# Attention joined to a mixture of experts: another order of work where the last heads meet the first expert

## The chip, the cores and the metric

The kernel runs on one core of one Trainium2 chip. The metric is the device time of one execution in microseconds. The engines of the core are TensorE (PE, and PEld for its weight loads), VectorE (DVE), ScalarE (ACT), GpSimd (POOL) and SyncE (SP); each executes its own instructions in the order in which they were written.

## The reference

Causal attention with a forgetting bias comes first, and its output rows are the input of eight experts, of which each row takes one:

```python
scores = scale * np.matmul(q, k.transpose(0, 1, 3, 2))          # q, k, v: 8 x 8 x 576 x 64
cum = np.cumsum(np.maximum(s, 0.0), axis=-1)
bias = -(cum[:, :, :, None] - cum[:, :, None, :])
scores = np.where(causal, -1000000000.0, scores + np.minimum(bias, 0.0))
attn = np.exp(scores - np.max(scores, axis=-1, keepdims=True))
attn = attn / (np.sum(attn, axis=-1, keepdims=True) + 1e-09)
x = np.matmul(attn, v).transpose(0, 2, 1, 3).reshape(4608, 512)
...
logits = xn @ en.T / tau                                        # normed rows, 8 experts
expert_idx = np.argmax(logits, axis=1)
gate_w = probs[np.arange(N), expert_idx]                        # softmax of the logits
for e in range(8):
    h = np.maximum(x[mask] @ w1[e], 0.0)                        # 512 -> 1024
    out[mask] = gate_w[mask, None] * (h @ w2[e])                # 1024 -> 512
```

## The kernel before

Every operand of a matmul that needs more than 16 bits is kept as a high and a low part, and each product is three matmuls. So an exponential P has a remainder PL (the function `pl_`, line 235 on POOL and line 488 on DVE), v has vh (ACT, line 292) and vl (DVE, line 293), a weight has a converted half (`wcv`, ACT, line 804) and a remainder (`wlow`, DVE, line 812), a row of x has xH (ACT, line 741) and xL (DVE, line 743), and the hidden layer has a Relu (ACT, line 833) and its remainder (DVE, line 834; its tiles are called hv, hp and hq).

**Attention** is a software pipeline, `step(n)`, one step for each of the 64 heads (NH = 64) and a few steps around them. Step n computes the scores of head n on PE (tiles ta and tb), their exponentials on ACT (`expa`, line 478, and `expb1`, line 481), the conversion of v, and the product P times v of head n - 2 (`pv`, 15 triples of matmuls, 128 x 73 each, into the PSUM tile om, lines 506 to 508). The three DVE instructions `norm1` to `norm3` (lines 519, 523, 531) divide om by the row sums into xt. There is one tile om, so `pv` of a head waits until `norm3` of the head before it has read om; `norm1` of head n - 3 stands at the beginning of step n.

After the last head of a batch the **router** (`router`, lines 575 to 659) picks each row's expert in a queue of small DVE tasks (`sume`, `sel1` to `sel5`), PE ranks the rows (`rank0`), DVE computes their places (`rank1` to `rank3`, `rows`), and POOL scatters the rows to the DRAM table xs (`scat`, line 645, five for a batch). `slot()` takes one task from the queue, `scatter()` one scatter.

**Experts**: `xload` gathers 128 rows from xs (POOL, line 705), `xprep` transposes them on PE (line 736, four matmuls) and splits them into xH and xL; `l1(m, e, lo, hi)` computes one of eight slices of the hidden layer (line 824), `l2(e, t)` one tile of 128 rows of the output (line 848, 24 matmuls). `l1` has two PSUM buffers: slice m + 2 waits until DVE has taken the remainder of slice m out of PSUM. `wsq` sums squares of weights on ACT (line 776), `wnorm` (lines 787 to 794) makes a scale from the sums with one matmul and six small DVE instructions, and raw weights arrive by DMA in tiles that `wlow` gives free. The first three row tiles of expert 0 (SPL = 384 rows) are known early; its other two tiles, t = 3 and 4, need the scatters of the last two batches.

**The joint** is steps 62 to 66 and the code behind them. In step 63 (n = NH - 1) come the transposes of the three early row tiles; `tail(n)` puts `l1(0)`, `l1(1)`, `l1(2)` into steps 64 to 66, ahead of `pv` of heads 62 and 63; then follow `l1(3)` to `l1(7)`, three `l2`, and within them `third` and `fourth` (the row tiles 3 and 4), and then the rest of expert 0, in which a second `gate` (lines 77 to 104: norm, logits, exps, weight) is computed after the slices m = 1, 3, 5 and 7. All order is that of the written code.

Of the kernel before, what the change touches and what calls it, by code (L numbers as in the profile page):

```python
# [106 lines left out]
def main(ctx, tc, qkh, qkc, vtin, s_in, emb, tau, w1h, w2h, out, shared, nb):  # L107
# [402 lines left out]
    def norm1(n):  # L510
        if not 0 <= n < NH:
            return
        b, hh = n // H, n % H
        o = HD[n]["o"]
        if hh == 0:
            XT[b] = p2.tile([128, 5, XR], F32, name="xt", bufs=2)
        z = HD[n]["z"] = p2.tile([128, 5], F32, name="z")
        ov = HD[n]["ov"] = o[:, 0:365].rearrange("p (j c) -> p j c", c=73)
        nc.vector.tensor_scalar(z, ov[:, :, 72 * (hh % 2)], 1.0e-9 * 2.0 ** PSH, 2.0 ** XSH, op0=ALU.add, op1=ALU.mult)

    def norm2(n):
        if 0 <= n < NH:
            nc.vector.reciprocal(HD[n]["z"], HD[n]["z"])

    def norm3(n):
        if not 0 <= n < NH:
            return
        b, hh = n // H, n % H
        xt, z, ov = XT[b], HD[n]["z"], HD[n]["ov"]
        o = 72 * hh  # L530
        nc.vector.tensor_tensor(xt[:, :, o:o + 72], ov[:, :, 1 - hh % 2:73 - hh % 2], z.unsqueeze(2).to_broadcast([128, 5, 72]), op=ALU.mult)  # L531
        del HD[n]
        if hh == H - 1:
            nc.gpsimd.tensor_copy(xt[:, :, XW:XR].bitcast(I32), IX["recf"][:, b].unsqueeze(2).to_broadcast([128, 5, XR - XW]))
            nc.gpsimd.tensor_copy(xt[:, :, XW + 1:XW + 3], VB[b]["ws"].unsqueeze(1).to_broadcast([128, 5, 2]))
            router(b, xt)
# [38 lines left out]
    def router(b, xt):  # L575
# [17 lines left out]
        def sel4():  # L593
            R["w"] = om[:, 500:505]
            nc.vector.tensor_reduce(R["w"], R["T"], AX.X, ALU.max)
# [122 lines left out]
    def xprep(e, t, pt=None, info=True):  # L718
# [3 lines left out]
        if e + t // (SPL // 128) > 0 and not isinstance(X[("L", e)], tuple):  # L722
            X[("L", e)] = (X[("L", e)], p2.tile([128, 4, CAP], F16, tag="xt", name="xL", bufs=2))
        x = X[("r", e, t)][:, 0:XW]
# [10 lines left out]
        for c in range(4):  # L735
            nc.tensor.transpose(out=pt[:, 128 * c:128 * c + 128], in_=x[:, 144 * c + 8:144 * c + 136], identity=ident)
        if info:
            xstat(e, t)
        pv = pt.rearrange("p (c t) -> p c t", c=4)
        xH = X[("H", e)][:, :, 128 * t:128 * t + 128]  # L740
        nc.scalar.copy(xH, pv)
        xL = X[("L", e)] if e + t // (SPL // 128) == 0 else X[("L", e)][1]
        nc.vector.tensor_tensor(xL[:, :, 128 * t:128 * t + 128], pv, xH, op=ALU.subtract)  # L743
# [65 lines left out]
    def wlow():  # L809
        while lows:  # L810
# [90 lines left out]
    def step(n):  # L901
# [70 lines left out]
        wlow()  # L972
# [25 lines left out]
        tail(n)  # L998
# [7 lines left out]
        if n == NH - 1:  # L1006
            xprep(0, 2, pxs(), False)
        pv(n - 2, [3, 4])
        if live:
# [10 lines left out]
        if live:  # L1020
            prep(n, False)
            if n:
                vcp(n, True)
        if k > 0:
# [3 lines left out]
        slots(4)  # L1028
# [8 lines left out]
        for _ in range(SCN[c8] if n < NH - 22 else 1 + (c8 > 5) + 4 * (n > NH - 6)):  # L1037
            scatter()
# [9 lines left out]
    def PS(n):  # L1048
        return 1600 if n < NH - 6 else 1024

    def tail(n):
# [16 lines left out]
        if k == 7:  # L1068
            for t in range(2):
                xprep(0, t, pxs(), False)  # L1070
# [31 lines left out]
    for m in range(3, 8):  # L1102
        l1(m, 0, 0, SPL, partial(some, 12) if m == 5 else wnorm if m == 4 else None)
        if m == 3:
            wlow()
            some(12)
# [4 lines left out]
        if m > 5:  # L1111
            some(0)
# [4 lines left out]
    xinfo(0, SPL // 128, NTL)  # L1117
    for t in range(SPL // 128, NTL):
        xload(0, t)
# [19 lines left out]
    l2(0, 1)  # L1139
    wsq(24)  # L1140
    l2(0, 2, {4: third, 7: fourth})
    for e in range(NE):
        nx = e + 1 < NE
        w2, w1 = 16 * e + 8, 16 * e + 16
        for m in range(8):
# [26 lines left out]
            if e == 0 and m % 2:  # L1172
                X[("g", 0, SPL // 128)][m // 2]()
# [162 lines left out]
```

## Time and profile before

| | |
|---|---|
| median of 3 runs | 790.39 us (789.15 to 791.65) |
| the profiled execution | 791.17 us, of which the span from the first to the last instruction is 789.5 us |
| PE busy | 764.2 us, 97% of the span |
| DVE, ACT, POOL busy | 527.9, 566.5, 382.8 us |
| TensorE's granted clock, mean | 0.991 of full speed |

A row of a timeline has the start of an instruction in us from the start of the span, its length, engine, line, operation, output and inputs, shape and count, and in brackets the idle time of the engine ahead of it with what ended it. Attention ends and the experts begin between 343 and 420 us.

### The profile page before, as it was taken

To read this page: it belongs to the slowest core of one execution; us is meant where nothing else is said; L and a number is where in the kernel's file an instruction comes from. 1 tells how busy PE (TensorE), PEld (TensorE's weight loads), DVE (VectorE), ACT (ScalarE), POOL (GpSimd) and SP (SyncE) were. 2 spreads that over 40 slices of the span, in tenths; PEclk is the share of its full clock that TensorE was granted. 3 is DMA by queue.
4 is the path that set the end of the run, shared out by engine and by line. 5 is a ranking of instruction groups with operands and counts; after the bars stand their busy time and mean duration, and the time that the engine had idled before them with its cause. 6 is when DMAs were issued, how large, how long until landed. Compare 5 with 4: busy or idle time off the path is not lost. (4 is left out here: it accounts for less than half of the span.)

```text
span 789.5 us, 19448 instructions
## 1 busy us (share of the span) xinstructions
PE 764.2 (97%) x7290; PEld 570.3 (72%) x7290; DVE 527.9 (67%) x1784; ACT 566.5 (72%) x1010; POOL 382.8 (48%) x369
## 2 busy tenths in 40 slices
PE   8799999999999999987999999999999999999997
PEld 4699999999999999975476647556465574664753
DVE  7767888888888888877565756555664565556621
ACT  6699989898989898966556866837747567476410
POOL 8767798989898979771432121230221212302001
PEclk9899999999999999999999999999999999999999
DMA  8897879797979796770635665564754657635001
GB/s 160 195 210 134 180 172 212 169 212 172 212 170 217 176 196 177 180 256 28 207 88 162 163 202 158 143 183 122 185 181 113 177 154 147 194 106 131 24 15 54
DMA packets 76896, 125.03 MB, mean 158 GB/s; under 512 B 38960, under 2 KB 39364, under 8 KB 75934
## 3 DMA queue, kind: packets, MB, share of 16 engines
q0 software_dynamic: 20240, 70.92, 38.5%
q1 hardware_dynamic: 56560, 52.84, 24.6%
q8 instruction: 58, 0.95, 0.5%
q14 instruction: 38, 0.31, 0.1%
HBM read 95.23 MB, written 21.49 MB: 148 GB/s over the span
## 5 line engine op out<-in xcount | busy, mean ns | idle before, releaser
L235 POOL TENSOR_TENSOR PL<-P 128x576 f16<-128x576 f32 (+2 forms) x128 | 203.4, 1695 | 19.0 <-ACT P L478 10.6
L824 PEld LDWEIGHTS <-wt 128*128 128x128 f16 x1536 | 150.0, 98 | 63.2 <-issue 4.8
L824 PE MATMUL h<-xH,wt 128*128 128x320 f16 (+2 forms) x1024 | 187.8, 299 | 2.5 <-DVE hq L834 1.8
L854 POOL DMA_INDIRECT out<-Kx,xj x39 | 40.3, 1034 | 162.5 <-DVE Kx L853 112.4
L705 POOL DMA_INDIRECT Qx<-xs,idx x40 | 43.2, 1080 | 143.7 <-ACT hp L833 84.8
L506 PE MATMUL om<-vh,P 128*128 128x73 f16 x960 | 107.9, 199 | 3.4 <-DVE xt L531 3.0
L508 PE MATMUL om<-vh,PL 128*128 128x73 f16 x960 | 107.1, 198 | 0.9 <-POOL PL L235 0.9
L507 PE MATMUL om<-vl,P 128*128 128x72 f16 x960 | 107.3, 197 | 0.0
L824 PE MATMUL h<-xL,wt 128*128 128x320 f16 (+1 forms) x480 | 106.1, 297 | 0.5 <-DVE xL L743 0.5
L343 PE MATMUL s<-qkb 96*128 96x288 f32 (+4 forms) x270 | 96.8, 372 | 2.3 <-DVE M L351 1.1
L507 PEld LDWEIGHTS <-P 128*128 128x128 bf16 x960 | 95.2, 99 | 4.5 <-issue 4.1
L508 PEld LDWEIGHTS <-PL 128*128 128x128 f16 x960 | 94.3, 98 | 1.2 <-POOL PL L235 1.2
L848 PE MATMUL pxs<-wt,hp 128*128 128x512 f16 x351 | 94.9, 379 | 0.0
L506 PEld LDWEIGHTS <-P 128*128 128x128 bf16 x960 | 94.2, 99 | 0.2
L848 PE MATMUL pxs<-wt,hq 128*128 128x512 f16 x351 | 88.6, 379 | 0.0
L351 DVE CUSTOM_DVE_ANT_0 junk<-s,mS 128x320 bf16<-128x320 f32 (+3 forms) x142 | 73.3, 524 | 4.9 <-PE s L343 3.4
L853 DVE TENSOR_SCALAR Kx<-pxs,xj,idx 128x512 f32<-128x512 f32 x39 | 31.5, 808 | 55.7 <-PE pxs L848 39.9
L481 ACT ACTIVATE P<-tb 128x1024 f32<-128x1024 f32 x64 | 65.2, 1018 | 3.5 <-PE tb L448 2.5
L445 PE MATMUL tb<-QC,KC 128*128 128x448 f32 (+3 forms) x256 | 64.3, 309 | 0.0
L848 PEld LDWEIGHTS <-hp 128*128 128x128 f16 x351 | 34.3, 98 | 41.5
L848 PEld LDWEIGHTS <-hq 128*128 128x128 f16 x351 | 34.3, 98 | 41.3
L833 ACT ACTIVATE hv<-h 128x640 f16<-128x640 f32 (+2 forms) x18 | 11.6, 645 | 72.6 <-PE h L824 63.4
(239 smaller groups left out, 1845.0 us busy)
## 6 DMA issues: line engine op xcount, KB each, us to landing
qkb<-qkh POOLq DMA_DIRECT2D x15, 1216.0 KB, 9.2
ring<-w2h SPq DMA_DIRECT2D x44, 256.0 KB
ring<-w1h SPq DMA_DIRECT2D x36, 256.0 KB
vT<-vtin SPq DMA_DIRECT2D x28, 320.0 KB
KC<-qkh POOLq DMA_DIRECT2D x15, 576.0 KB, 9.1
QC<-qkh POOLq DMA_DIRECT2D x15, 576.0 KB, 8.2
rw<-w1h SPq DMA_DIRECT2D x15, 256.0 KB
rw<-w2h SPq DMA_DIRECT2D x12, 256.0 KB
```

What stands on the lines that cost most here:

```text
L235: nc.gpsimd.tensor_tensor(out, a, b_, op=ALU.subtract)
L343: nc.tensor.matmul(out, G[g]["QB"][0:96, h, 128 * i:128 * i + 128], G[g]["KB"][0:96, h, lo:hi], start=True, stop=True)
L351: nc.vector.tensor_tensor_reduce(out=jk, in0=src, in1=ms, scale=1.0, scalar=NEG, op0=ALU.add, op1=ALU.max, accum_out=MP[n // 2][:, n % 2, ...
L445: nc.tensor.matmul(out, HD[n]["KC"][:, ks:ks + 128], HD[n]["QC"][:, qlo:qhi], start=False, stop=stop)
L481: nc.scalar.activation(HD[n]["P32"][:, 576:1600], HD[n]["tb"], AF.Exp, scale=0.125)
L506: nc.tensor.matmul(out, lh, vh[:, kb], start=(kb == 0), stop=False)
L507: nc.tensor.matmul(out[:, u:u + 72], lh, vl[:, kb], start=False, stop=False)
L508: nc.tensor.matmul(out, ll, vh[:, kb], start=False, stop=(kb == j))
L705: ins = nc.gpsimd.indirect_dma_start(out=x.bitcast(I32), out_offset=None, in_=src, in_offset=bass.IndirectOffsetOnAxis(ap=X[("i", e, t)][1 ...
L824: nc.tensor.matmul(h[:, u, 0:b - a], w[:, 128 * c:128 * c + 128], x[:, c, lo + a:lo + b], start=(c == 0 and k == 0), stop=(c == 3 and k == 2))
L848: nc.tensor.matmul(y, h[:, 128 * t:128 * t + 128], w, start=(m == 0 and k == 0), stop=(m == 7 and k == 2))
L854: nc.gpsimd.indirect_dma_start(out=out, out_offset=bass.IndirectOffsetOnAxis(ap=xf[0].bitcast(U32), axis=0), in_=ys, in_offset=None, bound ...
```

## The change

It rewrites the joint. In step 63 the second exponential of head 63, the conversion of v and the matmuls of `pv(61)` stand ahead of the row conversions (`xprep` is cut into `xtr`, the transposes, and `xcv`, the conversions). The norms of heads 61, 62 and 63 follow their own `pv` at once instead of standing in the next step. The weight remainders of steps 63 and 64 are taken together, four of them, behind the norm of head 62; those of steps 64 and 65 stand behind `l1(3)`. `PS` now gives all of the remainder PL of heads 62 and 63 to POOL; before, 576 of its 1600 columns were DVE's. The five scatters of batch 6 move from the end of step 62 to the end of step 64. `l1(0)` to `l1(2)` stand behind the `pv` of their step. The router of the last batch takes its tasks in steps 65 and 66 and inside `l1(3)`, not inside and behind `l1(3)` to `l1(5)`. Its PSUM columns move (500:505 to 496:501), so that they no longer overlap those of `wnorm`. The gathers of row tiles 3 and 4 stand behind `l1(4)` and `l1(5)`, `third` in the second `l2` and `fourth` earlier in the third one. The second gate's parts come after slices 1, 4, 5 and 7.

```diff
@@ -508,7 +508,7 @@
     def norm1(n):
-        if not 0 <= n < NH:
+        if n not in HD:
             return
...
@@ -591,7 +591,7 @@
             nc.vector.tensor_tensor(R["T"], R["T"], wval, op=ALU.mult)
 
         def sel4():
-            R["w"] = om[:, 500:505]
+            R["w"] = om[:, 496:501]
             nc.vector.tensor_reduce(R["w"], R["T"], AX.X, ALU.max)
 
         def sel5():
@@ -715,12 +715,29 @@
         nc.scalar.activation(P32J[:, 0:DM].rearrange("p (q d) -> p q d", q=4), x.rearrange("p (q c) -> p q c", q=4)[:, :, 8:136], AF.Square, accum_out=ss)
         esum(nc, L, x.unsqueeze(1))
 
-    def xprep(e, t, pt=None, info=True):
+    def xset(e, t):
         if ("H", e) not in X:
             X[("H", e)] = const.tile([128, 4, CAP], F16, tag=f"vT{e % 2}", name="xH")
             X[("L", e)] = WT[1][:, 8192:8192 + 4 * SPL].rearrange("p (c t) -> p c t", c=4)
         if e + t // (SPL // 128) > 0 and not isinstance(X[("L", e)], tuple):
             X[("L", e)] = (X[("L", e)], p2.tile([128, 4, CAP], F16, tag="xt", name="xL", bufs=2))
+
+    def xtr(e, t, pt):
+        xset(e, t)
+        x = X[("r", e, t)][:, 0:XW]
+        for c in range(4):
+            nc.tensor.transpose(out=pt[:, 128 * c:128 * c + 128], in_=x[:, 144 * c + 8:144 * c + 136], identity=ident)
+        X[("p", e, t)] = pt
+
+    def xcv(e, t):
+        pv = X[("p", e, t)].rearrange("p (c t) -> p c t", c=4)
+        xH = X[("H", e)][:, :, 128 * t:128 * t + 128]
+        nc.scalar.copy(xH, pv)
+        xL = X[("L", e)] if e + t // (SPL // 128) == 0 else X[("L", e)][1]
+        nc.vector.tensor_tensor(xL[:, :, 128 * t:128 * t + 128], pv, xH, op=ALU.subtract)
+
+    def xprep(e, t, pt=None):
+        xset(e, t)
         x = X[("r", e, t)][:, 0:XW]
         if e > 1:
             if "xr" not in HT:
@@ -732,15 +749,9 @@
             for o, r in ((X[("H", e)], h), (X[("L", e)][1], l)):
                 nc.sync.dma_start_transpose(o[:, :, 128 * t:128 * t + 128], r.rearrange("p q c -> p (q c)"))
             return xstat(e, t)
-        for c in range(4):
-            nc.tensor.transpose(out=pt[:, 128 * c:128 * c + 128], in_=x[:, 144 * c + 8:144 * c + 136], identity=ident)
-        if info:
-            xstat(e, t)
-        pv = pt.rearrange("p (c t) -> p c t", c=4)
-        xH = X[("H", e)][:, :, 128 * t:128 * t + 128]
-        nc.scalar.copy(xH, pv)
-        xL = X[("L", e)] if e + t // (SPL // 128) == 0 else X[("L", e)][1]
-        nc.vector.tensor_tensor(xL[:, :, 128 * t:128 * t + 128], pv, xH, op=ALU.subtract)
+        xtr(e, t, pt)
+        xstat(e, t)
+        xcv(e, t)
 
     def pxm():
         return ps_m.tile([128, 512], F32, tag="m", name="pxm")
@@ -806,8 +817,8 @@
         if not hold:
             wlow()
 
-    def wlow():
-        while lows:
+    def wlow(k=99):
+        for _ in range(min(k, len(lows))):
             q, l, a, s, h = lows.popleft()
             nc.vector.scalar_tensor_tensor(l, a, s, h, op0=ALU.mult, op1=ALU.subtract)
             wissue(q + 15)
@@ -969,7 +980,8 @@
         mslot()
         if prev and PS(n) < 1600:
             pl_(n - 1, PS(n), 1600, "v")
-        wlow()
+        if n < NH - 1:
+            wlow()
         k = n - NH + 8
         if k > 7:
             wsq((12, 14, 16)[k - 8])
@@ -995,7 +1007,8 @@
         if n > 1:
             sb(m)
             sbr(m)
-        tail(n)
+        if n < NH:
+            tail(n)
         pv(n - 2, [0, 1, 2])
         if rq:
             rq.popleft()()
@@ -1003,9 +1016,15 @@
             s4(m)
         if n < 0:
             heat(2)
-        if n == NH - 1:
-            xprep(0, 2, pxs(), False)
         pv(n - 2, [3, 4])
+        if n >= NH:
+            for f in (norm1, norm2, norm3):
+                f(n - 2)
+            if n == NH:
+                wlow(4)
+            for _ in range(9 if n == NH + 2 else 2):
+                slot()
+            tail(n)
         if live:
             expb1(n)
             if n:
@@ -1021,11 +1040,19 @@
             prep(n, False)
             if n:
                 vcp(n, True)
+        if n == NH - 1:
+            xcv(0, 0)
+            for f in (norm1, norm2, norm3):
+                f(n - 2)
+            for t in range(1, 3):
+                xtr(0, t, pxs())
+                xcv(0, t)
         if k > 0:
             wsq((0, 2, 3, 6, 8, 8, 9, 10, 12, 14, 16)[k])
             wcv((0, 0, 0, 0, 0, 1, 2, 2, 1, 2, 0)[k], True)
         brk[0] = False
-        slots(4)
+        if n < NH:
+            slots(4)
         if live and 2 <= c8 < 6 and b1 < nb:
             vsq(b1, (c8 - 2,))
         if live and c8 == 6 and b1 < nb:
@@ -1034,7 +1061,7 @@
             loadt(b1, c8)
         if n == NH - 8:
             wissue(3)
-        for _ in range(SCN[c8] if n < NH - 22 else 1 + (c8 > 5) + 4 * (n > NH - 6)):
+        for _ in range(SCN[c8] if n < NH - 22 else 0 if NH - 3 < n < NH else 1 + (c8 > 5) + 4 * (n > NH - 6)):
             scatter()
         later()
         if live and c == (n < HG):
@@ -1046,7 +1073,7 @@
             pl_(n, 0, 576, "p")
 
     def PS(n):
-        return 1600 if n < NH - 6 else 1024
+        return 1024 if NH - 7 < n < NH - 1 else 1600
 
     def tail(n):
         k = n - NH + 8
@@ -1066,8 +1093,7 @@
             for t in range(3):
                 xload(0, t)
         if k == 7:
-            for t in range(2):
-                xprep(0, t, pxs(), False)
+            xtr(0, 0, pxs())
         if 8 <= k < 11:
             l1(k - 8, 0, 0, SPL)
 
@@ -1100,23 +1126,23 @@
     for n in range(1 - LA, NH + 3):
         step(n)
     for m in range(3, 8):
-        l1(m, 0, 0, SPL, partial(some, 12) if m == 5 else wnorm if m == 4 else None)
+        l1(m, 0, 0, SPL, partial(some, 12) if m == 3 else wnorm if m == 4 else None)
         if m == 3:
             wlow()
-            some(12)
         if m > 3:
             wcv((2, 1, 2, 2)[m - 4])
         if m < 6:
             xstat(0, m - 3)
-        if m > 5:
-            some(0)
+        if m == 4:
+            some(4)
+            xinfo(0, SPL // 128, NTL)
+            xload(0, 3)
+        if m == 5:
+            xload(0, 4)
         if m == 7:
             for f in X[("g", 0, 0)][0:2]:
                 f()
     assert not (mq or tasks or first or late or scats)
-    xinfo(0, SPL // 128, NTL)
-    for t in range(SPL // 128, NTL):
-        xload(0, t)
     xinfo(1, 0, NTL)
     xload(1, 2)
 
@@ -1136,9 +1162,9 @@
     wsq(18)
     l2(0, 0, {3: opening})
     wsq(21)
-    l2(0, 1)
+    l2(0, 1, {4: third})
     wsq(24)
-    l2(0, 2, {4: third, 7: fourth})
+    l2(0, 2, {2: fourth})
     for e in range(NE):
         nx = e + 1 < NE
         w2, w1 = 16 * e + 8, 16 * e + 16
@@ -1169,8 +1195,8 @@
             if e == 0 and m in (3, 6):
                 xprep(1, m // 3 - 1, (pxm, pxs)[m // 3 - 1]())
                 xload(1, 2 + m // 3)
-            if e == 0 and m % 2:
-                X[("g", 0, SPL // 128)][m // 2]()
+            if e == 0 and m in (1, 4, 5, 7):
+                X[("g", 0, SPL // 128)][(1, 4, 5, 7).index(m)]()
             if e > 0 and m < 4:
                 X[("g", e, 0)][m]()
             if not nx and m == 5:
```

Line numbers below are those of each kernel; in the changed one 736, 741 and 743 have become 729, 735 and 737, and 776, 804, 812, 833, 834 have become 787, 815, 823, 844, 845.

On DVE, from the end of step 62 into the code behind step 65, these instructions stood in this order (vl is the remainder of v, wt a converted weight tile or, from pxs, the low part of rows, z and xt the norms, hv and hp the hidden layer's remainders):

```order
L293 SCALAR_TENSOR_TENSOR vl<-V,sc,vh_107 128x3x144
...
L488 TENSOR_TENSOR PL_110<-P_87 128x576
L812 SCALAR_TENSOR_TENSOR wt<-rw_196,idx,wt 128x512
...
L743 TENSOR_TENSOR wt<-pxs,xH 128x4x128 x3
L293 SCALAR_TENSOR_TENSOR vl<-V,sc,vh_107 128x2x144
L519 TENSOR_SCALAR z<-om 128x5
...
L488 TENSOR_TENSOR PL_108<-P_85 128x576
L812 SCALAR_TENSOR_TENSOR wt<-vh_106,idx,wt 128x512 x2
L834 SCALAR_TENSOR_TENSOR hv<-h,hv 128x384
L519 TENSOR_SCALAR z<-om 128x5
```

and now, from the same vl on (left out are the norm of head 60, the rest of each norm, and one weight remainder):

```order
L293 SCALAR_TENSOR_TENSOR vl<-V,sc,vh_107 128x3x144
...
L293 SCALAR_TENSOR_TENSOR vl<-V,sc,vh_107 128x2x144
L737 TENSOR_TENSOR wt<-pxs,xH 128x4x128
L519 TENSOR_SCALAR z<-om 128x5
...
L737 TENSOR_TENSOR wt<-pxs,xH 128x4x128 x2
L519 TENSOR_SCALAR z<-om 128x5
...
L823 SCALAR_TENSOR_TENSOR wt<-rw_196,idx,wt 128x512
...
L823 SCALAR_TENSOR_TENSOR wt<-vh_106,idx,wt 128x512 x2
L845 SCALAR_TENSOR_TENSOR hv<-h,hv 128x384
L519 TENSOR_SCALAR z<-om 128x5
...
L74 TENSOR_REDUCE om<-xt 128x40
```

The two PL parts have left DVE, the norms stand ahead of the weight remainders, and the router's first task (L74) stands right behind the last head's norm.

On POOL the scatters of batch 6 stood between the PL parts of heads 61 (PL_109) and 62 (PL_110):

```order
L705 DMA Qx<-xs,idx 128x580 x3
L235 TENSOR_TENSOR PL_109<-P_86 128x576
L235 TENSOR_TENSOR PL_109<-P_86 128x448
L645 DMA xs<-xt,pos 36864x580 x5
L235 TENSOR_TENSOR PL_110<-P_87 128x576
L235 TENSOR_TENSOR PL_110<-P_87 128x448
L235 TENSOR_TENSOR PL_108<-P_85 128x576
L235 TENSOR_TENSOR PL_108<-P_85 128x448
L534 COPY xt<-idx 128x5x4
```

Now they stand behind those of head 63 (PL_108), whose second parts have 1024 columns:

```order
L705 DMA Qx<-xs,idx 128x580 x3
L235 TENSOR_TENSOR PL_109<-P_86 128x576
L235 TENSOR_TENSOR PL_109<-P_86 128x448
L235 TENSOR_TENSOR PL_110<-P_87 128x576
L235 TENSOR_TENSOR PL_110<-P_87 128x1024
L235 TENSOR_TENSOR PL_108<-P_85 128x576
L235 TENSOR_TENSOR PL_108<-P_85 128x1024
L645 DMA xs<-xt,pos 36864x580 x5
L534 COPY xt<-idx 128x5x4
```

Nothing else moves on POOL up to the last batch's scatters; behind them gathers and output scatters alternate in another order.

On DVE behind `l1(3)`, before (idx and xj are small tables; the first row is the remainder of slice 3, the last that of slice 4):

```order
L834 SCALAR_TENSOR_TENSOR hp<-h,hp 128x384
L588 TENSOR_TENSOR om<-om,rm 128x40
...
L599 TENSOR_TENSOR oh<-wsel,om 128x40
L712 SCALAR_TENSOR_TENSOR xj<-Qx,idx 128x1
...
L788 TENSOR_REDUCE idx<-om 128x1
...
L794 TENSOR_TENSOR idx<-idx 128x1
L834 SCALAR_TENSOR_TENSOR hq<-h,hq 128x384
```

and now:

```order
L845 SCALAR_TENSOR_TENSOR hp<-h,hp 128x384
L823 SCALAR_TENSOR_TENSOR wt<-rv,idx,wt 128x512 x2
L823 SCALAR_TENSOR_TENSOR wt<-mS,idx,wt 128x512
L712 SCALAR_TENSOR_TENSOR xj<-Qx,idx 128x1
...
L799 TENSOR_REDUCE idx<-om 128x1
...
L805 TENSOR_TENSOR idx<-idx 128x1
L845 SCALAR_TENSOR_TENSOR hq<-h,hq 128x384
```

The router's tasks have gone from there, and three weight remainders have come in.

## Rows read from the trace of the kernel before

**Rows 1.** Busy time by stretch: length, each engine, granted clock, DMA share, GB/s.

```profile
343.17:376.06 32.89, 27.04 (x279) 19.17 (x276) 26.37 (x66) 20.86 (x48) 12.61 (x13) 0.95 0.32 101
376.06:419.48 43.42, 40.50 (x247) 24.16 (x246) 25.64 (x83) 26.97 (x70) 14.59 (x15) 1.00 0.50 161
419.48:780.00 360.52, 360.52 (x2182) 212.15 (x2181) 202.52 (x493) 212.77 (x486) 68.32 (x67) 1.00 0.50 138
359.00:363.00 4.00, 3.89 (x50) 3.27 (x50) 2.29 (x7) 3.71 (x10) 0.00 (x0) 0.57 0.00 0
```

**Rows 2.** Whom PE waited for, 343 to 376 us, then 376 to 430 us.

```profile
PE om L506 <- DVE xt L531: 2.6, 1, 2.6
PE om L787 <- DVE oh L599: 1.0, 1, 1.0
...
PE h L824 <- DVE hq L834: 1.3, 1, 1.3
PE h L824 <- ACT xH L741: 0.7, 1, 0.7
```

**Rows 3.** DVE's timeline, 340 to 359 us.

```profile
340.92 0.75 DVE L488 TENSOR_TENSOR PL<-P 128x576 f16<-128x576 f32 x1
...
348.85 0.69 DVE L743 TENSOR_TENSOR wt<-pxs,xH 128x512 f16<-128x512 f32 x1 [0.77 <-issue]
...
351.47 4.23 DVE L488 TENSOR_TENSOR PL<-P 128x576 f16<-128x576 f32 x1
355.62 1.40 DVE L812 SCALAR_TENSOR_TENSOR wt<-vh,idx,wt 128x512 f16<-128x512 f32 x2
...
358.11 0.15 DVE L519 TENSOR_SCALAR z<-om 128x5 f32<-128x5 f32 x1
...
358.53 0.53 DVE L531 TENSOR_TENSOR xt<-om,z 128x360 f32<-128x360 f32 x1
```

**Rows 4.** POOL's timeline, 344 to 356 us.

```profile
344.31 1.58 POOL L645 DMA_INDIRECT xs<-xt,pos  x1 [3.44 <-DVE z L523]
...
351.00 4.07 POOL L235 TENSOR_TENSOR PL<-P 128x576 f16<-128x576 f32 x4
```

**Rows 5.** ACT's timeline, 348 to 363 us.

```profile
348.23 0.59 ACT L741 CAST xH<-pxs 128x512 f16<-128x512 f32 x1 [0.98 <-PE pxs L736]
348.71 1.03 ACT L481 ACTIVATE P<-tb 128x1024 f32<-128x1024 f32 x1
...
357.12 0.49 ACT L833 ACTIVATE hv<-h 128x384 f16<-128x384 f32 x1 [3.79 <-DVE wt L812]
...
362.58 0.20 ACT L778 CAST idx<-idx 128x8 bf16<-128x8 f32 x1
```

**Rows 6.** Stretches as in rows 1, each cut at one group of instructions.

```profile
445.58:450.76 5.18, 5.18 (x26) 2.35 (x24) 2.65 (x7) 4.92 (x13) 0.55 (x1) 1.00 0.97 214
341.67:343.15 1.48, 1.48 (x47) 1.48 (x45) 1.04 (x2) 1.48 (x4) 0.00 (x0) 1.00 0.39 151
345.53:346.40 0.87, 0.87 (x10) 0.86 (x9) 0.79 (x2) 0.23 (x1) 0.56 (x2) 1.00 0.00 0
354.39:356.34 1.95, 1.95 (x17) 1.18 (x14) 1.95 (x3) 0.00 (x0) 1.89 (x3) 1.00 0.05 17
368.13:369.60 1.47, 1.33 (x9) 0.82 (x10) 1.30 (x10) 0.06 (x1) 0.00 (x0) 1.00 0.00 0
372.32:373.51 1.19, 1.19 (x8) 0.66 (x7) 1.09 (x10) 1.14 (x3) 0.00 (x0) 1.00 0.75 203
402.71:404.46 1.75, 0.91 (x9) 0.67 (x7) 1.47 (x10) 0.41 (x2) 0.93 (x1) 1.00 0.18 21
```

**Rows 7.** POOL's and DVE's timelines, 373 to 391 us: scatter, gather, landing.

```profile
373.96 1.01 POOL L645 DMA_INDIRECT xs<-xt,pos  x1 [17.55 <-DVE idx L640]
...
386.38 1.05 POOL L705 DMA_INDIRECT Qx<-xs,idx  x1 [6.15 <-DMA xs<-xt,pos]
...
389.96 0.16 DVE L712 SCALAR_TENSOR_TENSOR xj<-Qx,idx 128x1 int32<-128x1 int32 x1 [2.21 <-DMA Qx<-xs,idx]
```

More of the change, by code (lines that the diff above doesn't have):

```diff
@@ L521, in norm2 @@
     def norm2(n):
-        if 0 <= n < NH:
+        if n in HD:
             nc.vector.reciprocal(HD[n]["z"], HD[n]["z"])
     def norm3(n):
-        if not 0 <= n < NH:
+        if n not in HD:
             return
```

## The prediction, made before the changed kernel was run

> **What bounds the kernel now.** I began with the page's table: PE is busy 97% of the span, so time comes off only where PE stands still or is clocked down. The busy times by stretch show where [rows 1]. From 419.48 us on PE is busy for all of the 360.52 us up to 780, so whatever arrives earlier there shortens the end by as much. Between 343.17 (step 63 begins) and 376.06 (the first `l2`) PE is busy for 27.04 of 32.89 us, and between 376.06 and 419.48 for 40.50 of 43.42. The granted clock falls only in the first: 0.57 on average over 359 to 363, so most of that at the lower level, 1.2 GHz, behind PE's longest pause.
>
> Next I asked whom PE waited for [rows 2]. The largest wait, 2.6 us, is of `pv(63)` for the norm of head 62; then 1.3 and 1.0 us on DVE, and 0.7 us for the conversion of the late row tile. Third, what DVE did ahead of that norm: one L488 took 4.23 us where the same instruction takes 0.75 [rows 3], and in those 4 us POOL ran four L235 in a row, 351.00 to 355.07 [rows 4]. DVE's instruction ended only after POOL's last. Behind it stood two weight remainders (1.40 us) that read the tile into which ACT had to write hv, so ACT stood for 3.79 us [rows 5], then hv, then the norm. POOL was late because five scatters, waiting for the gathers ahead of them, held it from 344.31 to 351.00 [rows 4].
>
> **The first stretch, from parts.** PE's work there, each length from first start to next start: 2.36 us of scores and v up to the transposes at 345.53; 0.87 for eight of twelve transposes, so 0.44 for four; 1.48 for the 45 matmuls of a `pv`; 1.95 for the 12 of an `l1` [rows 6]. With three `pv` (4.4), eight `l1` (15.6), 1.3 for transposes and 0.3 (estimate) for the eleven small matmuls of rank and norm that is 24.0 of 32.89 us. So 8.9 us are lost before the change: 5.85 of idle time, 1.7 by the clock (four us at 0.57 of full speed), and the rest because idle time is counted from the modelled end of a matmul, which lies some 0.15 to 0.2 us behind the start that its successor could have had.
>
> What the new order waits for, walked along PE with the same lengths:
> - Step 63. Transposes of tile 0 end at 345.97, `pv(61)` at 347.45. The last exponential no longer stands behind three row conversions: it can start when its matmuls end (about 345.3), takes 1.03, v's conversion 0.4 (estimate, a smaller one than the 0.59 of a row conversion), the row conversion 0.59 and its DVE part 0.69 [rows 3, 5]: 348.05. The third transposes need that buffer: a wait of 0.2. Then the norm of head 61, 0.95 from its first start to its last end [rows 3], 348.95: `pv(62)` waits 0.4 and runs to 350.4.
> - POOL now computes PL of heads 62 and 63 with no scatters ahead. The 576 extra columns twice are 2 x 0.9 us at most (the four parts of 576 and 448 columns took 4.07, about 1 each), and PL(63) is done near 348.5, four us before `pv(63)` wants it. So this part costs nothing; if POOL were three us later it would cost the excess.
> - Norm of 62 at 351.4; `l1(0)` covers it. Then four weight remainders, 2.8 us (1.40 for two), to 354.2; hv on ACT to 354.75, its remainder and the norm of 63 by 356.3. Meanwhile `pv(63)`, `l1(1)` and `l1(2)` run to 357.8. That hv remainder is needed by `l1(2)` at 355.9: covered by 0.6. The 2.6 us wait and the clock's fall are gone. In the trace of before `l1(2)` ends near 364.1.
> - ACT is the next limit: from the start of hv to the end of the sums' cast it needs 5.66 us (357.12 to 362.78) [rows 5], now 354.4 to 360.1. The Relu of slice 2 stands behind it, and `l1(4)`, ready at 360.2, needs its remainder at 361.3: a wait of 1.1.
> - Then DVE: 1.19 for the rank [rows 6] ahead of hp delays the weight remainders, so `l1(5)` waits about 0.35 for one of them; between the remainders of slices 3 and 4 stand three weight remainders (2.0), and 1.47 for statistics and scale [rows 6], together 3.5 us against 1.95 of matmuls: `l1(6)` waits about 1.2. Two waits of 0.1 besides.
>
> New waits: 0.2 + 0.4 + 1.1 + 0.35 + 1.2 + 0.2 = 3.45. The first `l2` starts at 343.17 + 24.0 + 3.5 = 370.7: 5.4 us sooner. The bounds: no wait at all would give 8.9; twice my waits, 2.0.
>
> One cost is not in this. In step 62 POOL's first part for head 62 can now start as head 61's ends, at about 340.9, where DVE starts L488 (340.92) and then a weight remainder. In the trace of before such an L488 behind four parts of POOL took 4.23 instead of 0.75 us [rows 3, 4]. Here, unlike there, POOL has one ready and the next only when its exponential ends, so the delay of DVE is between 0 and about 3.3 us; the norm of head 60, which `pv(61)` needs, has 2 to 1.1 us of slack. So 0 to 2.2; I take 0.7, between an immediate slip into POOL's gap and one further part waited for. The Trainium skill, "SBUF — State Buffer", section "Who interferes with whom", says that a DVE instruction with two SBUF inputs and a GpSimd instruction that reads SBUF exclude each other for the whole of the one that started first; the 4.23 us above agree. By that rule alone, with POOL first each time, the 2.2 would be due.
>
> **The second stretch.** Five waits, 2.92 us of idle time [rows 1], or about 3.8 from start to start.
> - The router ends sooner. Its rank tasks now follow slice 2's remainder at about 361, 1.19 us long, so the first scatter is at 362.5 to 363.2. Before, the first landing came 16.0 us behind the first scatter (373.96 to 389.96) [rows 7]: now 378.8 to 379.5. PE reaches the third tile's transposes one `l2` (5.18 us for 24 matmuls) and 15 matmuls (3.2) behind 370.7 to 371.4 [rows 6]: 379.2 to 379.9. So the data are there with 0.4 us to spare, the transposes no longer end just ahead of the slices that need them, and about 1.9 us from start to start (0.7 and two smaller waits) vanish.
> - The gate: nine logits instructions, 1.75 us [rows 6], stood with a row conversion between the remainders of slices 3 and 4, and PE waited 1.3 us [rows 2]. One slice later they have no row conversion ahead. Slice 4's remainder, at 403.2 in the old count, makes `l1(6)` in time; slice 5's comes at 405.3 against 405.2: 1.2 of 1.3 us saved.
> - The other two short waits (0.3 to 0.5) stay.
>
> Saved 3.1 us, between 0 (late landing) and 3.8.
>
> **The sum.** 5.4 - 0.7 + 3.1 = 7.8. The sum is made against 791.17 us, the profiled execution's own time, 0.78 above the median of the runs: 783.4 there, 782.6 at the median. I say 783.0.
>
> **The rivals.** A difference under 0.3% (2.4 us) can't be told from none.
> 1. *As summed*: 781 to 785. For it: every length above is a row of this trace. Chance 0.60.
> 2. *No new waits in `l1(3)` to `l1(7)`*: if ACT and DVE find their work earlier than I place it, 2.7 us more go: 780.3. DVE's 26.37 us of work in 32.89 [rows 1] lose 4.2 with L488, and 22 in 27.5 leaves room; against it: the pieces between two remainders are longer than an `l1`. Chance 0.11.
> 3. *DVE behind POOL in step 62, and again where the remainders and PL meet*: `pv(61)` 2.2 us late and another 1 to 2 us later: 785 to 787.5. For it the 4.23 us; against it, POOL has a gap there. Chance 0.16. The rule of the Trainium skill's "SBUF — State Buffer", section "Who interferes with whom", taken at its full price, would lead here.
> 4. *The wait moves*: the same DVE and ACT work decides the joint, and the waits double: 788 to 791, no difference. Chance 0.08.
> 5. *Slower: the gather behind `third`.* `third` stands one `l2`, 5.2 us of PE work, earlier, and PE waits in order. If the data land no sooner than before, at 389.96, PE waits 10.8 us for them from 379.2 on and is then 5.2 us behind the old order, of which the 3.1 us of the second stretch come back: 793.3. It is even with before when they land at 387.9, over 8 us behind my estimate, and slower by 2.4 us from 390.3 on (later scatters, or ones that land more slowly). Against it: the rank tasks stand ahead of slice remainders that PE needs anyway. Chance 0.05.
>
> **How the numbers follow.** Faster 0.60 + 0.11 + 0.16 = 0.87, same 0.08, slower 0.05. The range reaches from rival 2 to the upper end of rival 3, 780.3 to 787.5, and leaves out rivals 4, 5 and part of 2, under 0.2.
>
> **What would show it.** Right: no wait for L531 above 0.6 us; granted clock 1.00 from 356 to 366; POOL's parts for heads 62 and 63 end before 349 with no scatter between; the first `l2` at 370 to 372; waits of about a us on ACT or DVE at the fifth and seventh `l1`; first scatter of the last batch at 362 to 364; no wait for a gather; expert 1 starting near 411.7 instead of 419.48, and no idle time behind. Wrong: an L488 or weight remainder of over 1.5 us in step 62, a wait for the gather in the second `l2`, idle time behind expert 1's start, or a new fall of the clock.

## The result, and the profile of the changed kernel

The changed kernel took 783.32 us (median of 4 runs, 782.95 to 785.43) beside 790.26 us of the kernel before: a ratio of 0.9906, with a 95% interval of 0.9885 to 0.9926. The profiled execution took 783.26 us, its span 781.4. In two later sets of runs on one chip PE stood still for up to 4.2 us beside the scatters, as it did in no other set; the changed kernel took 790.07 us there (see "A pause that is in none of the edits"), and times of these two sets are compared only among themselves.

Busy time by stretch, as in [rows 1]: step 63 to the first `l2`, from there to expert 1, the rest, and the part in which the clock had fallen:

```profile
342.79:370.55 27.76, 25.07 (x279) 17.78 (x276) 23.34 (x65) 20.63 (x48) 14.52 (x15) 1.00 0.46 158
370.55:410.73 40.18, 39.88 (x247) 24.34 (x246) 25.90 (x83) 26.85 (x71) 11.56 (x11) 1.00 0.46 147
410.73:772.00 361.27, 360.67 (x2181) 212.13 (x2180) 202.62 (x493) 212.80 (x486) 68.32 (x67) 1.00 0.51 138
356.00:366.00 10.00, 8.28 (x60) 4.77 (x58) 7.73 (x31) 6.17 (x17) 2.88 (x3) 1.00 0.38 140
```

The first stretch is 5.13 us shorter than before (32.89), the second 3.24 (43.42), and the granted clock stays at 1.00, its upper level, 2.4 GHz. Two differences belong to neither: step 63 begins 0.38 us sooner, of which 0.3 stands in the trace from 82 us on and the rest from 286 us on, long before the change, and a later expert has a new wait of 0.6 us, a matmul of `wnorm` for ACT's cast:

```profile
666.46 0.17 PE L798 MATMUL om<-idx,onesb 128*128 128x8 bf16 x1 [0.60 <-ACT idx L789]
```

5.13 + 3.24 + 0.38 - 0.65 (that wait, from start to start) = 8.10, the difference of the spans. Of six kernels below with the same code there, four don't wait and two wait 0.4 us, so this is counted as scatter between runs and not as an effect of the change.

Whom PE waited for from 342 to 411 us (total, times, longest; `l1` is L835 here, `l2` L859), beside [rows 2]:

```profile
PE h L835 <- DVE hq L845: 2.2, 2, 1.3
PE V L282 <- DVE vl L293: 0.3, 1, 0.3
PE pxs L859 <- DVE wt L823: 0.2, 1, 0.2
```

The 2.6 us for the norm are gone, and so is all that had stood in the second stretch but 0.2 us. The two waits for hq are those of the fifth and the seventh `l1`:

```profile
361.01 0.32 PE L835 MATMUL h<-xH,wt 128*128 128x384 f16 x1 [0.84 <-DVE hq L845]
366.45 0.32 PE L835 MATMUL h<-xH,wt 128*128 128x384 f16 x1 [1.33 <-DVE hq L845]
```

This list goes by the modelled end of the matmul before, so it leaves one wait out: the weight load ahead of `pv(62)` waits for the norm of head 61, and the first matmul of `pv(62)` starts about 0.3 us later than it could (0.42 us behind the last transpose, where transposes follow each other every 0.11).

```profile
348.90 0.10 PEld L506 LDWEIGHTS <-P 128*128 128x128 bf16 x1 [0.38 <-DVE xt L531]
```

DVE's timeline (as [rows 3]; L823 is the weight remainder, L845 that of the hidden layer) and POOL's (as [rows 4, 7]):

```profile
340.54 1.68 DVE L488 TENSOR_TENSOR PL<-P 128x576 f16<-128x576 f32 x1
342.14 2.38 DVE L823 SCALAR_TENSOR_TENSOR wt<-rw,idx,wt 128x512 f16<-128x512 f32 x1
344.44 0.66 DVE L293 SCALAR_TENSOR_TENSOR vl<-V,sc,vh 128x432 f16<-128x432 f32 x1
...
345.43 0.53 DVE L531 TENSOR_TENSOR xt<-om,z 128x360 f32<-128x360 f32 x1
...
350.62 0.17 DVE L519 TENSOR_SCALAR z<-om 128x5 f32<-128x5 f32 x1 [0.35 <-PE om L508]
...
354.84 0.56 DVE L845 SCALAR_TENSOR_TENSOR hv<-h,hv 128x384 f16<-128x384 f32 x1 [0.62 <-ACT hv L844]
```

```profile
338.46 3.14 POOL L235 TENSOR_TENSOR PL<-P 128x576 f16<-128x576 f32 x3
341.92 2.05 POOL L235 TENSOR_TENSOR PL<-P 128x1024 f16<-128x1024 f32 x1 [0.33 <-ACT P L481]
344.81 3.12 POOL L235 TENSOR_TENSOR PL<-P 128x576 f16<-128x576 f32 x2 [0.84 <-ACT P L478]
348.09 1.03 POOL L645 DMA_INDIRECT xs<-xt,pos  x1 [0.16 <-DVE z L519]
...
362.51 0.99 POOL L645 DMA_INDIRECT xs<-xt,pos  x1 [7.68 <-DVE idx L640]
...
372.64 1.04 POOL L705 DMA_INDIRECT Qx<-xs,idx  x1 [4.08 <-ACT idx L82]
```

POOL's parts end at 347.93, ahead of the norms of heads 62 and 63 (350.62 and 355.32). The 4.23 us instruction is gone; in its place, one step sooner, DVE's L488 takes 1.68 and the weight remainder 2.38 us where each takes 0.75 alone. ACT (as [rows 5]) writes hv 2.8 us sooner, and slice 2's Relu comes 5.56 us behind it:

```profile
344.93 1.02 ACT L481 ACTIVATE P<-tb 128x1024 f32<-128x1024 f32 x1 [0.20 <-PE tb L448]
...
354.32 0.49 ACT L844 ACTIVATE hv<-h 128x384 f16<-128x384 f32 x1 [1.68 <-DVE wt L823]
...
359.88 0.48 ACT L844 ACTIVATE hq<-h 128x384 f16<-128x384 f32 x1
```

The late rows land 1.5 us ahead of the transposes that read them (DVE's first read of them, and PE):

```profile
377.80 0.16 DVE L712 SCALAR_TENSOR_TENSOR xj<-Qx,idx 128x1 int32<-128x1 int32 x1 [0.35 <-DMA Qx<-xs,idx]
```

```profile
379.34 0.60 PE L729 MATMUL pxm<-ident,Qx 128*128 128x128 f32 x4
```

### The profile page after: what moved, and what is told of

Same layout as the page of the kernel before. It is cut to its first block, busy times and chain, and to the rows that moved or that the text cites. A ratio compares the mean times of both kernels' runs of the same rounds, so it can differ in the third digit from the quotient of the medians.

```text
span 781.4 us, 19445 instructions
## 1 busy us (share of the span) xinstructions
PE 762.0 (98%) x7290; PEld 568.9 (73%) x7290; DVE 525.6 (67%) x1782; ACT 566.1 (72%) x1010; POOL 383.3 (49%) x369
## 5 line engine op out<-in xcount | busy, mean ns | idle before, releaser
L835 PEld LDWEIGHTS <-wt 128*128 128x128 f16 x1536 | 149.7, 98 | 62.1 <-issue 2.9
L835 PE MATMUL h<-xH,wt 128*128 128x320 f16 (+2 forms) x1024 | 187.2, 299 | 2.2 <-DVE hq L845 2.2
L835 PE MATMUL h<-xL,wt 128*128 128x320 f16 (+1 forms) x480 | 106.1, 297 | 0.0
L859 PE MATMUL pxs<-wt,hp 128*128 128x512 f16 x351 | 94.9, 379 | 0.0
L859 PE MATMUL pxs<-wt,hq 128*128 128x512 f16 x351 | 88.7, 379 | 0.0
L859 PEld LDWEIGHTS <-hq 128*128 128x128 f16 x351 | 34.3, 98 | 41.3
L859 PEld LDWEIGHTS <-hp 128*128 128x128 f16 x351 | 34.2, 98 | 41.3
L445 PE MATMUL tb<-QC,KC 128*128 128x448 f32 (+3 forms) x256 | 63.7, 307 | 0.0
```

The costliest lines, as they stand in the source:

```text
L445: nc.tensor.matmul(out, HD[n]["KC"][:, ks:ks + 128], HD[n]["QC"][:, qlo:qhi], start=False, stop=stop)
L835: nc.tensor.matmul(h[:, u, 0:b - a], w[:, 128 * c:128 * c + 128], x[:, c, lo + a:lo + b], start=(c == 0 and k == 0), stop=(c == 3 and k == 2))
L859: nc.tensor.matmul(y, h[:, 128 * t:128 * t + 128], w, start=(m == 0 and k == 0), stop=(m == 7 and k == 2))
```

## The experiments

Each is the changed kernel with one edit, except where it says otherwise. "Joint" is the time from the first L445 matmul of step 63 to the first `l2`, 27.38 us in the changed kernel and 32.51 before; "second stretch" goes from there to expert 1, 40.18.

**The gate's place.**

```diff
-            if e == 0 and m in (1, 4, 5, 7):
-                X[("g", 0, SPL // 128)][(1, 4, 5, 7).index(m)]()
+            if e == 0 and m % 2:
+                X[("g", 0, SPL // 128)][m // 2]()
```

> The changed kernel with the gate's last parts back at slices 1, 3, 5 and 7 of expert 0. Theory (the term of 1.2 us in the second stretch): the nine logits instructions stand again ahead of slice 4's remainder on DVE, and one wait of 1.2 to 1.3 us for it comes back at the seventh l1 of expert 0; expert 1 starts 1.2 us later behind the first l2, 784.5 us in all. Rival: the late tile's conversions, moved elsewhere by the same change, had already freed DVE there, so the old place costs at most 0.3 us: 783.3 to 783.6.

784.58 us (783.46 to 784.84); joint 27.40, second stretch 41.60, 1.42 longer. PE's waits behind 370 us show the one wait back:

```profile
PE h L835 <- DVE hq L845: 1.3, 1, 1.3
```

The term of 1.2 us holds.

**The late tiles' transposes.**

```diff
-    l2(0, 1, {4: third})
+    l2(0, 1)
     wsq(24)
-    l2(0, 2, {2: fourth})
+    l2(0, 2, {4: third, 7: fourth})
```

> The changed kernel with the transposes of the fourth and fifth row tile back in the third l2 (after its slices 3 and 7); the router, the scatters and the gathers stay early. Theory (the term of 1.9 us): the two short waits for the row conversion, 0.7 and 0.5 us idle time or 1.2 to 1.9 us from start to start, come back at expert 0's first l1, 784.5 to 785.2 us. Rival: those waits were caused by the late data alone, and with the data there early the old place costs nothing: 783.3 us.

784.68 us (783.97 to 786.73); joint 27.37, second stretch 41.68, 1.50 longer, with the waits of [rows 2] back although the rows were there:

```profile
PE h L835 <- ACT xH L735: 0.7, 1, 0.7
PE h L835 <- DVE xL L737: 0.5, 1, 0.5
```

So it was the place of the transposes, not the data.

**The router late, the transposes early.** The loop over `l1(3)` to `l1(7)` is that of the kernel before:

```diff
-        l1(m, 0, 0, SPL, partial(some, 12) if m == 3 else wnorm if m == 4 else None)
+        l1(m, 0, 0, SPL, partial(some, 12) if m == 5 else wnorm if m == 4 else None)
...
+    xinfo(0, SPL // 128, NTL)
+    for t in range(SPL // 128, NTL):
+        xload(0, t)
```

> The changed kernel with the router's last rank tasks back in the sixth l1 and the gathers of the late tiles back behind all eight, while the transposes of the fourth tile stay in the second l2: the case in which the gather stands behind its reader. Theory: before the change the late rows landed 13.9 us behind the first l2, and PE reaches their transposes 8.8 us behind it, so PE waits about 5.1 us for the gather, once: 788 to 789 us, expert 1 starting about 5 us later than in the changed kernel. Rival: with no scatters held up in front, they land 3 us sooner than before and PE waits 1 to 2 us: 784.5 to 785.5 us. Second rival: no wait, 783.3 us.

784.94 us (784.58 to 786.92). That lies in the first rival's range, but neither theory nor rival came about: PE waited for no gather. The first late rows were read at 381.32, 2 us ahead of PE (383.29), and the second stretch is 40.15. The time went in the joint, 30.87, which is 3.5 us longer. PE's wait for the rank, then two stretches around it:

```profile
PE om L798 <- DVE pos L627: 2.1, 1, 2.1
```

```profile
360.00:364.00 4.00, 1.76 (x19) 0.91 (x16) 3.12 (x6) 1.80 (x7) 0.00 (x0) 0.99 0.00 0
364.00:368.00 4.00, 3.27 (x12) 1.58 (x13) 2.65 (x17) 1.04 (x3) 1.97 (x2) 0.50 0.19 74
```

The rank tasks stand behind three weight remainders on DVE, the matmul of `wnorm` waits for their last read, and behind that the clock falls to 1.2 GHz. This trace is of the slowest of the four runs (786.92); the other three took 784.58 to 785.17 us with a mean clock of 0.994 or 0.995, as the changed kernel has, so a fall of the clock is shown for this one run alone, and without it the late router costs about 1.5 us. What the router's place sets is the joint, not the gather.

**The weight remainder of step 62.** It is done with the four of step 64 (`n < NH - 2`, `wlow(5)`).

> The changed kernel without the weight remainder in step 62; it is done with the four others in step 64. Theory: the remainder took 2.38 us there instead of 0.75 because POOL's multiplication ran, but this delay of DVE reached PE only as the 0.3 us wait for v's remainder; that wait vanishes, while 0.7 us more of DVE work now stands ahead of the first Relu's store and passes on to the wait at the fifth l1: 783.2 to 783.8 us. Rival: the delay of DVE cost as much as the prediction took, 0.7 us or more, so the kernel gains 0.7 to 1.5 us: 781.8 to 782.6 us.

783.03 us (782.79 to 783.67). Without it DVE is 2 us sooner at v's remainder and the norm of head 60:

```profile
340.64 1.68 DVE L488 TENSOR_TENSOR PL<-P 128x576 f16<-128x576 f32 x1
342.49 0.67 DVE L293 SCALAR_TENSOR_TENSOR vl<-V,sc,vh 128x432 f16<-128x432 f32 x1 [0.17 <-ACT vh L292]
343.08 0.17 DVE L519 TENSOR_SCALAR z<-om 128x5 f32<-128x5 f32 x1
```

PE's 0.3 us wait for v's remainder is gone, and `pv(62)` starts 0.45 us sooner in the joint. But the joint is 27.88, 0.5 longer: the remainder is needed in `l1(0)` already, where PE now waits for it, while the wait at the fifth `l1`, which was expected to grow, shrinks to 0.3.

```profile
PE h L835 <- DVE wt L823: 1.4, 1, 1.4
```

The delay of DVE in step 62 thus costs PE 0.3 us of idle time, 0.5 from start to start. The time itself, 783.03 beside 783.32 us, is too close to tell.

**A pause that is in none of the edits.** Four kernels ran together in the next set: the scatters of batch 6 back in steps 62 and 63, POOL's 576 columns of heads 62 and 63 back on DVE, and two meant to be faster.

```diff
-        for _ in range(SCN[c8] if n < NH - 22 else 0 if NH - 3 < n < NH else 1 + (c8 > 5) + 4 * (n > NH - 6)):
+        for _ in range(SCN[c8] if n < NH - 22 else 1 + (c8 > 5) + 4 * (n > NH - 6)):
```

> The changed kernel with the five scatters of the last batch but one back in steps 62 and 63, ahead of POOL's parts of heads 62 and 63 (each now 1600 columns, 3.1 us). Theory: the scatters hold POOL from about 344.3 to 351.0 as before, the two heads' parts end near 354.1 and 357.2, and the last but one value product, which starts at 348.9 in the changed kernel, waits about 4 to 5 us for the first; the clock may fall behind that. 787.5 to 789.5 us, and most of the gain of the first stretch is gone. Rival: what counted was the exponential ahead of the row conversions; POOL's order is covered and costs at most 1 us: 783.3 to 784.3 us.

```diff
-        return 1024 if NH - 7 < n < NH - 1 else 1600
+        return 1600 if n < NH - 6 else 1024
```

> The changed kernel with 576 columns of heads 62 and 63 back on DVE (0.75 us each alone); the scatters stay behind. Theory: DVE has about a us to spare ahead of the norms, but each of these stands beside a POOL part, as the 1.68 and 2.38 us instructions of step 62 do in the changed kernel, so DVE loses 2 to 4 us in steps 63 and 64 and PE 0.5 to 2 us: 783.8 to 785.3 us. Rival: POOL was merely late before, DVE's halves fit, and the shift of columns to POOL bought nothing: 783.3 us.

```diff
-            wsq((12, 14, 16)[k - 8])
+            wsq((12, 14, 14)[k - 8])
...
             tail(n)
+            if n == NH + 2:
+                wsq(16)
```

> The changed kernel with the last two squares of a weight and their sum's conversion on ACT behind the Relu of slice 2 instead of ahead of it (1.8 us of ACT work). Theory: that Relu ended 1.4 us late by them; the wait of 0.84 us at the fifth l1 vanishes, DVE's run of remainders starts up to 1.4 us sooner, and the wait of 1.3 us at the seventh l1 shrinks to about 0.9: 782.0 to 782.5 us. Rival: the sums' matmul in the middle of the fifth l1 now waits for that conversion instead, and nothing is gained: 783.3 us.

```diff
         if m == 3:
-            wlow()
+            wlow(2)
```

> As the run before (squares behind the Relu of slice 2), and of the three weight remainders between the fourth and the fifth slice's remainders on DVE only two, the third behind the fifth slice's. Theory: DVE between the two slices is the whole of the wait at the seventh l1, so it shrinks by the 0.7 us of a remainder to about 0.2: 781.3 to 781.8 us. Rival: the remainder put off stands ahead of the next slice's instead and PE waits for it at the eighth l1: no gain over the run before.

789.78, 789.49, 788.17 and 788.72 us: none as expected, though the last two don't touch an instruction ahead of the pause. In the last three PE stands still for 4.1 to 4.2 us in step 64. The first kernel, whose scatters run in steps 62 and 63, from 344.13 to 350.29, has no such pause in step 64, against what the next expectation says of all four; there PE stops in step 63 instead, 1.9 us in three waits without a named cause ("issue"):

```profile
PE om L508 <- issue: 1.2, 1, 1.2
```

So the changed kernel itself was run again, with the kernel before in POOL's part alone.

> The changed kernel itself, once more, beside the others. In the four kernels run last a pause of PE of 4 to 5 us stands in step 64 between the end of one value product (its semaphore comes that much behind its last matmul) and the norm, with nothing but scatters and weight loads running; none of their edits but the one on POOL's scatters touches an instruction ahead of it. If the pause belongs to the edits, the changed kernel is again without it: 783.3 us and 27.4 us from step 63 to the first second-layer matmul. If it belongs to when or where they ran, it shows here too: about 788 us and 32 us.

790.07 us (788.77 to 793.33), ratio 0.9978 (0.9954 to 1.0003), joint 33.44: the pause belongs to where and when they ran, and not to these edits. What is left of the gain there, 1.3 us, can't be told from none. The kernel before took 791.00 and 791.33 us in these two sets, no more than the 791.58 us of the earlier set on the same chip, so by its times the old order doesn't lose by it; no trace of it is there to show why. DVE's and POOL's timelines and two stretches of this run:

```profile
350.48 1.29 DVE L737 TENSOR_TENSOR wt<-pxs,xH 128x512 f16<-128x512 f32 x2
357.07 0.17 DVE L519 TENSOR_SCALAR z<-om 128x5 f32<-128x5 f32 x1 [5.31 <-remote]
```

```profile
349.73 1.03 POOL L645 DMA_INDIRECT xs<-xt,pos  x1 [0.16 <-DVE z L519]
...
354.95 0.93 POOL L645 DMA_INDIRECT xs<-xt,pos  x1 [0.30 <-issue]
```

```profile
354.00:358.00 4.00, 0.25 (x2) 0.03 (x1) 0.86 (x4) 0.14 (x2) 1.97 (x4) 0.86 0.52 176
358.00:362.00 4.00, 3.92 (x49) 3.32 (x49) 3.35 (x8) 1.23 (x3) 0.00 (x0) 0.50 0.46 137
```

PE's last recorded matmul of `pv(62)` begins at 351.89, but the norm that reads it begins at 357.07, released by something that the trace doesn't name ("remote"), while scatters run; then the clock is at 0.50. In the undisturbed trace the same norm begins 0.23 us behind the start of that matmul (350.39 to 350.62), beside the same scatters, so these alone don't make the pause. Against this run, the scatters' old place (joint 32.33) and DVE's columns (33.02, each L488 again 0.75 us in steps 63 and 64) cost nothing that can be told; what they cost without the pause stays open. The two squares moved save 0.68 us from the last `pv` to the first `l2` (20.17 to 19.49), and with the remainder put off 0.82: as the rival of that run says, its wait has mostly moved, from 1.0 at the seventh `l1` to 0.4 there and 0.7 at the eighth.

> The kernel before with POOL's part of the change alone: the five scatters go behind the parts of heads 62 and 63, and POOL takes all 1600 columns of these. Theory: DVE's 4.23 us instruction and the lateness of POOL are gone, and with them the 2.6 us wait for the norm of head 62 and the fall of the clock behind it (1.7 us); the waits that come from ACT's and DVE's order stay: 786.5 to 788.5 us. Rival: POOL can't start head 63 before the last exponential, which still stands behind three row conversions, so the wait only changes its releaser: 789.5 to 790.5 us.

```diff
-        for _ in range(SCN[c8] if n < NH - 22 else 1 + (c8 > 5) + 4 * (n > NH - 6)):
+        for _ in range(SCN[c8] if n < NH - 22 else 0 if NH - 3 < n < NH else 1 + (c8 > 5) + 4 * (n > NH - 6)):
...
-        return 1600 if n < NH - 6 else 1024
+        return 1024 if NH - 7 < n < NH - 1 else 1600
```

791.66 us beside 791.33 of the kernel before in the same set. Its trace has the 2.6 us wait for the norm down to 0.6, and its joint is 30.42, but PE pauses without a named cause in `pv` (`issue` waits, 1.4 us), again beside the scatters. If the pauses only lengthen a joint, at least 2.1 of its 5.1 us are POOL's part; the rest of that part's worth can't be told from it, and its time shows no gain at all. What the exponential ahead of the row conversions and the norms at once are worth by themselves has no run of its own: it is read from the traces.

**The scatters out of the way.** A small copy that reads the sum of head 63 stands ahead of the five scatters on POOL:

```diff
+            if n == NH + 1:
+                nc.gpsimd.tensor_copy(p2.tile([128, 5], F32, name="zc", bufs=1), HD[n - 2]["z"])
...
-        for _ in range(SCN[c8] if n < NH - 22 else 0 if NH - 3 < n < NH else 1 + (c8 > 5) + 4 * (n > NH - 6)):
+        for _ in range(SCN[c8] if n < NH - 22 else 0 if NH - 3 < n < NH + 1 else 1 + (c8 > 5) + 4 * (n > NH - 6)):
```

> The changed kernel with the five scatters of the last batch but one held back on POOL until the norm of head 63 has begun (a small copy that reads its sum stands ahead of them), so that they run from about 355.6 to 362 us, beside matmuls of the first expert layer instead of the last two value products. Theory: the pause of 4 to 5 us, which in five traces began and ended with the transfers of these scatters while a value product stood on PE, belongs to that meeting; it is gone, and with it the fall of the clock: 783.3 to 784.5 us and 27.4 to 28.2 us from step 63 to the first second-layer matmul. Rival: the transfers stop PE whatever it runs; the pause stands in the second to fourth l1 now: 787 to 790 us.

783.42 us (783.18 to 784.25), joint 27.39. This set ran on another chip, and nothing shows that the changed kernel would have paused there: the run shows that the scatters can wait for 9 us (358.86 instead of 348.09, in a run whose step 63 begins 1.9 us later) at no cost that can be told, and doesn't settle the pause.

> The same, and in addition the two squares behind the Relu of slice 2 and the third weight remainder behind the fifth slice's. Theory: without the pause these two take the waits of 0.84 and 1.3 us at the fifth and seventh l1 down to 0.7 us together, as they did behind the pause (0.8 us from the last value product to the first second-layer matmul): 781.8 to 782.6 us. Rival: the pause stays, and this kernel is 0.8 us ahead of the other one at 786 to 789 us.

782.89 us (782.56 to 785.86), 0.53 below the run before, too little to tell. The joint is 26.08, 1.3 shorter, with the fifth `l1`'s wait gone, the seventh's at 0.4 and a new one of 0.7 at the eighth; but PE is now ahead of the gather, which stands behind the held scatters:

```profile
379.18 0.66 PE L729 MATMUL pxm<-ident,Qx 128*128 128x128 f32 x4 [0.46 <-DMA Qx<-xs,idx]
```

The second stretch is 40.78, 0.6 longer, so half of the gain is given back. The same edits without the held scatters had no run without the pause.

## Why the prediction was right, point by point

- **First stretch: 5.4 less 0.7 for step 62 predicted, 5.13 measured.** The causes of the old wait (POOL late, L488 behind it, the exponential behind row conversions) went as written: the exponential starts at 344.93, POOL ends head 63 at 347.93, the norm of 62 at 351.6. ACT's 5.66 us from hv to the end of the sums' cast were right, and with them the wait at the fifth `l1`: from start to start, as the prediction counts, 1.0 (1.1); the seventh's is 1.5 (1.2). The wait of `pv(62)` for the norm of head 61 came too, 0.3 of 0.4.
- **Waits that did not come**: 0.2 for the buffer of the third transposes, and 0.35 for a weight remainder at the sixth `l1`, where PE loses 0.02.
- **Step 62: the delay was right, its price too high.** DVE lost 2.6 us (1.68 + 2.38 against 1.50), inside the 0 to 3.3. The norm of head 60 ends at 345.96 and `pv(61)` begins at 346.18, so the slack took it all; PE's 0.3 us (0.5 from start to start) came at v's remainder, a reader that the prediction doesn't name. I took 0.7. The Trainium skill, "SBUF — State Buffer", section "Who interferes with whom", agrees with what DVE lost here (each instruction ends behind POOL's, as in [rows 3, 4]); the 2.2 us for PE that I derived from it by putting POOL first each time did not come.
- **Second stretch: 3.1 predicted, 3.24 measured.** Undone one by one, transposes and gate give 1.50 (I took 1.9) and 1.42 (1.2). The rest, 0.3, fits the 0.2 us wait for a gather that the trace before had and this one hasn't. That the total fits better than its two terms is luck: one was taken too high, the other too low. The prediction also counts six waits where the trace before has five: two that vanish beside the 0.7, and two that stay. Only one stayed, 0.2 for a weight remainder; the 0.5 was for xL of a late tile, and went with the transposes. From the first scatter to the late rows' read it took 15.3 us (16.0), and the scatter came at 362.51 (362.5 to 363.2).
- **The router: the step that I had the wrong way round.** I counted its 1.19 us on DVE as a cost of 0.35 and its place as a matter of the gather (rival 5: 10.8 us of waiting). With the router late, PE waits 2.1 us in the joint, in the traced run it loses clock behind it, and the gather is in time: the joint is longer too, so PE comes to the rows later.
- **The sum** was 7.8; the two stretches gave 8.37, the spans 8.10, and the medians 6.94, since the execution profiled before was slower than its median and the one profiled now wasn't. Rivals 2, 4 and 5 did not occur; of rival 3 the delay of DVE in step 62 did, but not its price.
- **Two signs of being wrong did show**: an L488 and a weight remainder of over 1.5 us in step 62 (1.68 and 2.38), and idle time behind expert 1's start (0.6). The first was meant to show the price of step 62, but a delay on DVE doesn't show what PE pays for it; the second is the wait counted above as scatter.
- **What no case had**: the pause. With it the gain is about 1 us, and the clock falls again, which was a sign of being wrong too.

## What to carry to other kernels

Walk the joint between two stages along the engine that is the bound, with measured lengths, and price a late neighbour by the slack of its reader, not by its own delay: 2.6 us lost on DVE cost PE 0.3 to 0.5. A small chain of tasks that feeds a transfer much later can also hold up a matmul close by; look for whoever waits on its last read before moving it. A list of waits that goes by modelled ends can miss one that shows in the weight loads. Run the same kernel again before you believe an experiment whose edit stands behind the place that changed.

## What the runs showed of the hardware

- A norm on DVE was released 5 us behind the last recorded matmul that it waits for. All ten runs of that set took 788.8 us or more; on the same chip an earlier set of four kernels had no such pause. Its cause is open. All six traces of the two disturbed sets have fewer records of semaphore updates than the eight others (755 to 761 of ACT's, where those have 806 or 807), and not only near the pause; whether what loses the records also holds PE isn't shown. The pauses stand beside indirect DMAs, and with the scatters in their old place PE stopped in step 63 and not in step 64; yet the last batch's scatters run beside `l1` in the same traces without one.
- Two DVE instructions of 0.75 us that met POOL's multiplications took 1.68 and 2.38 us beside one part each, and one took 4.23 beside four [rows 3, 4].
- The granted clock fell to the lower level behind PE's idle time, in the late router's run and in the paused one, and the matmuls behind it pay: in the paused run the last `pv` took 2.67 us from its first to its last start instead of 1.49.
